# Loads that cast to bf16 in the DMA, transposes of contiguous blocks, and an output phase two batches behind, in an attention and MoE kernel

## The chip, the cores and the metric

The kernel runs on one core of a Trainium2 chip. The metric is the device time of one execution in microseconds (us). A core has these engines: PE (TensorE, matmuls), DVE (VectorE), ACT (ScalarE), POOL (GpSimd) and SP (SyncE, which here only issues DMAs). 16 DMA engines move data for all of them. Executions of the kernel before mostly lie between 346 and 353 us. Some runs fell in a slow state, most of them with a lower granted PE clock; ratios leave them out, but for one, and the medians quoted count every run.

## The reference, cut to what matters

```python
batch, n_heads, seq, head_dim = (8, 8, 576, 64);  n_pack = 32
def sm_attn(qq, kk, vv):                       # softmax attention
    s = scale * np.matmul(qq, kk.transpose(0, 1, 3, 2))
    s = s - np.max(s, axis=-1, keepdims=True)
    a = np.exp(s)
    a = a / (np.sum(a, axis=-1, keepdims=True) + 1e-09)
    return np.matmul(a, vv)
p_packed = sm_attn(p, k, v)                    # 32 packed rows attend to 576 tokens
out = sm_attn(q, p_packed, p_packed)           # 576 tokens attend to the 32 rows
# ... x is out as (4608, 512)
h = x @ w_in                                   # 512 -> 2048
g = h * np.cos(h)
return g @ w_out                               # 2048 -> 512, fp32
```

Inputs and output are fp32; q, k and v are 1.18 MB per batch each. The kernel computes in bf16. It folds the second attention into w_in: PPW = p_packed @ w_in (32 rows per head), so h is the normalised weights a2n times PPW.

## The kernel before: the parts that the argument touches

A stage is one pass of the loop over batches. Stage s does the second attention of batch s (`s2`, `sums2`, `normalise`), the first attention of batch s + 1 (`s1`, a transpose of its weights a1 to a1T, `pp`, `ppw`), the h phase of batch s, and output matmuls of batch s - 1, spread as filler for PE (`fill(n)` emits n of them). The transposes of k, q and a1 go through DMA transposes that SP issues in program order. Tokens lie as `(p c)`: 96 partitions with 6 tokens each.

```python
raw_pool = ctx.enter_context(tc.tile_pool(name="raw", bufs=3))
def load(n, b, eng):                           # fp32, as it lies in memory
    t = raw_pool.tile([TP, H, C * D], FP32, name="raw", tag="raw")
    eng.dma_start(out=t, in_=srcs[n][b].rearrange("h (p c) d -> p h (c d)", c=C))
    raws[n, b] = t
def cast(n, b, eng, c0=0, c1=C):               # to bf16, (h c) -> (c h)
    ...
def xbar(n, b):                                # DMA transpose of q or k
    t = new_xT(n, b)
    nc.sync.dma_start_transpose(out=t.rearrange("p c a x -> p (c a) x"),
                                in_=bf[n, b].rearrange("p c x -> p (c x)"))
# ... cut
for s in range(1, B):
    nxt = s + 1 < B
    if s > 1:
        set_filler(s - 1)
        nc.scalar.preload_act_table_set(EXP_SET)
    s2(s)
    fill(7)
    if nxt:
        s1(s + 1)
        a1_xbar(s + 1)
        xbar("q", s + 1)
        if s + 2 < B:
            if ("k", s + 2) not in bf:
                cast("k", s + 2, G)
            xbar("k", s + 2)
    fill(3)
    sums2(s, 0)
    # ... cut
    for n, b in loads:                         # v and q of s + 2, k of s + 3
        load(n, b, G)
    # ... cut: 16 x h_mm; pp at 4, ppw at 7 and 11; casts on POOL at 8, 11, 14
set_filler(B - 1)
fill(1000)
```

The softmax here doesn't subtract the row's maximum and nothing guards it: scores larger than these inputs give would overflow.

Of the kernel before, what the change touches and what calls it, by code (L numbers as in the profile page):

```python
# [15 lines left out]
def kernel(  # L16
# [10 lines left out]

# [13 lines left out]
    raw_pool = ctx.enter_context(tc.tile_pool(name="raw", bufs=3))  # L41
    bf_pool = ctx.enter_context(tc.tile_pool(name="bf", bufs=1))
    att_pool = ctx.enter_context(tc.tile_pool(name="att", bufs=1))
    a2n_pool = ctx.enter_context(tc.tile_pool(name="a2n", bufs=2))
    ppw_pool = ctx.enter_context(tc.tile_pool(name="ppw", bufs=2))
    g_pool = ctx.enter_context(tc.tile_pool(name="g", bufs=2))
# [7 lines left out]
    ctx.enter_context(tc.manual_schedule())  # L54

# [5 lines left out]
    P2 = const.tile([128, B, 4, NP], BF16, name="P2")  # L61
# [3 lines left out]
    ppT = [const.tile([128, 4, NP], BF16, name=f"ppT{i}") for i in range(2)]  # L65
# [3 lines left out]
    raws, bf, xT, a1T, sums1, r1, rs1 = {}, {}, {}, {}, {}, {}, {}  # L69
    a2u, lns, a2n, PPW = {}, {}, {}, {}  # L70

# [3 lines left out]
    def load(n, b, eng):  # L75
        t = raw_pool.tile([TP, H, C * D], FP32, name="raw", tag="raw")
        eng.dma_start(out=t, in_=srcs[n][b].rearrange("h (p c) d -> p h (c d)", c=C))
        raws[n, b] = t

    def cast(n, b, eng, c0=0, c1=C):  # L80
        if (n, b) not in bf:
            bf[n, b] = bf_pool.tile([TP, C, H * D], BF16, name=n + "bf", tag=n + "bf", bufs=2 if n == "v" else 1)
        sv = raws[n, b].rearrange("p h (c d) -> p c h d", c=C)[:, c0:c1]
        dv = bf[n, b].rearrange("p c (h d) -> p c h d", h=H)[:, c0:c1]
        if eng is nc.scalar:
            nc.scalar.copy(out=dv, in_=sv)
        else:
            eng.tensor_copy(out=dv, in_=sv)  # L88

    def new_xT(n, b):  # L90
        xT[n, b] = att_pool.tile([128, C, 4, TP], BF16, name=n + "T", tag=n + "T")
        return xT[n, b]

    def xbar(n, b):
        t = new_xT(n, b)
        nc.sync.dma_start_transpose(out=t.rearrange("p c a x -> p (c a) x"),
                                    in_=bf[n, b].rearrange("p c x -> p (c x)"))

    def pe_T(n, b, i, eng):
        if i == 0:  # L100
            new_xT(n, b)
        ps = psa(BF16)
        for j in range(2):
            for hp in range(4):
                o = (j * 4 + hp) * TP
                nc.tensor.transpose(ps[:, 0, o:o + TP],
                                    bf[n, b][:, 2 * i + j, hp * 128:(hp + 1) * 128], ident[0:TP, 0:TP])
        dst = xT[n, b][:, 2 * i:2 * i + 2].rearrange("p c a x -> p (c a x)")
        sv = ps[:, 0, 0:8 * TP]
        if eng is nc.scalar:  # L110
            nc.scalar.copy(out=dst, in_=sv)
        else:
            nc.vector.tensor_copy(out=dst, in_=sv)

    def pack_p(b0, b1):
        n = b1 - b0
        ps = psa(BF16)
        flat = ps.rearrange("p a x -> p (a x)")
        for g in range(2 * n):
            nc.tensor.transpose(flat[:, g * 128:(g + 1) * 128],  # L120
                                p_bf[:, 2 * b0 + g].rearrange("p t d -> p (t d)"), ident)
        v4 = flat[:, 0:2 * n * 128].rearrange("p (a o n) -> p a o n", o=2, n=NP)
        dst = P2[:, b0:b1].rearrange("p b a x -> p (b a) x")
        nc.vector.tensor_copy(out=dst[0:64], in_=v4[0:64, :, 0, :])
        nc.vector.tensor_copy(out=dst[64:128], in_=v4[64:128, :, 1, :])

    def scores(lhs, rhs):
        ps = [psa(), psa()]
        for half in range(2):
            for hp in range(4):  # L130
                for par in range(2):
                    r = slice(64 * par, 64 * par + 64)
                    nc.tensor.matmul(ps[par][32 * hp:32 * hp + 32, half, 0:HS], lhs[r, hp, :],  # L133
                                     rhs[r, 3 * half:3 * half + 3, hp, :], start=True, stop=True)
        return ps

    def s1(b):
        ps = scores(P2[:, b], xT["k", b])
        sums1[b] = small.tile([128, 2], FP32, name="sums1")
        for par in range(2):  # L140
            nc.scalar.activation(  # L141
                out=a1[b % 2][:, par, :, 0:TP].rearrange("p (t c) x -> p t c x", t=2),
                in_=ps[par][:, :, 0:HS].rearrange("p t (c x) -> p t c x", c=3),
                func=AF.Exp, scale=scale, accum_out=sums1[b][:, par:par + 1])
        r1[b] = small.tile([128, 2], FP32, name="r1")
        rs1[b] = small.tile([128, 2], FP32, name="rs1")
        nc.vector.reciprocal(r1[b], sums1[b])  # L147
        nc.vector.tensor_scalar(out=rs1[b], in0=r1[b], scalar1=scale, scalar2=None, op0=ALU.mult)

    def new_a1T(b):  # L150
        a1T[b] = att_pool.tile([128, 2, C, 128], BF16, name="a1T", tag="a1T")
        return a1T[b]

    def a1_xbar(b):
        t = new_a1T(b)
        nc.sync.dma_start_transpose(out=t.rearrange("p a c x -> p (a c) x"),
                                    in_=a1[b % 2].rearrange("p a c x -> p (a c x)"))

    def a1_pe(b, engs):
        t = new_a1T(b)  # L160
        ps = psa(BF16)
        for par in range(2):
            for c in range(C):
                nc.tensor.transpose(ps[0:TP, par, c * 128:(c + 1) * 128], a1[b % 2][:, par, c, 0:TP], ident)
            dst = t[0:TP, par].rearrange("p c x -> p (c x)")
            sv = ps[0:TP, par, 0:C * 128]
            if engs[par] is nc.scalar:
                nc.scalar.copy(out=dst, in_=sv)
            else:
                nc.vector.tensor_copy(out=dst, in_=sv)  # L170

    def pp(b):
        ps = psa()
        for hp in range(4):
            for c in range(C):
                nc.tensor.matmul(ps[:, 0, hp * 64:(hp + 1) * 64], bf["v", b][:, c, hp * 128:(hp + 1) * 128],  # L176
                                 a1T[b][0:TP, :, c, 32 * hp:32 * hp + 32], start=(c == 0), stop=(c == C - 1))
        pv = ps[:, 0, 0:256].rearrange("p (a x) -> p a x", a=4)
        t = ppT[b % 2]
        nc.vector.tensor_copy(out=t[0:64], in_=pv[0:64, :, 0:32])  # L180
        nc.vector.tensor_copy(out=t[64:128], in_=pv[64:128, :, 32:64])

    def ppw(b, n0, cnt, engs):
        if b not in PPW:
            PPW[b] = ppw_pool.tile([128, 2, DF], BF16, name="PPW", tag="PPW")
        ps = [psa(), psa()]
        for j in range(cnt):
            for hp in range(4):
                for par in range(2):
                    r = slice(64 * par, 64 * par + 64)  # L190
                    nc.tensor.matmul(ps[par][32 * hp:32 * hp + 32, j, :], ppT[b % 2][r, hp, :],  # L191
                                     w_in_bf[r, hp, (n0 + j) * 512:(n0 + j + 1) * 512], start=True, stop=True)
        for par in range(2):
            dst = PPW[b][:, par, n0 * 512:(n0 + cnt) * 512].rearrange("p (j x) -> p j x", j=cnt)
            sv = ps[par][:, 0:cnt, :]
            if engs[par] is nc.scalar:
                nc.scalar.activation(out=dst, in_=sv, func=AF.Copy, scale=r1[b][:, par:par + 1])  # L197
            else:
                nc.vector.tensor_scalar(out=dst, in0=sv, scalar1=r1[b][:, par:par + 1], scalar2=None, op0=ALU.mult)  # L199

    def s2(b):
        a2u[b] = att_pool.tile([128, 2, S], BF16, name="a2u", tag="a2u")
        ps = scores(ppT[b % 2], xT["q", b])
        for par in range(2):
            nc.scalar.activation(out=a2u[b][:, par].rearrange("p (t x) -> p t x", t=2),
                                 in_=ps[par][:, :, 0:HS], func=AF.Exp, scale=rs1[b][:, par:par + 1])

    def sums2(b, par):
# [3 lines left out]
        for half in range(2):  # L212
            nc.tensor.matmul(ps[:, half, 0:HS], ones_blk, a2u[b][:, par, half * HS:(half + 1) * HS],
                             start=True, stop=True)
        nc.scalar.activation(out=lns[b][:, par].rearrange("p (t x) -> p t x", t=2),
                             in_=ps[:, :, 0:HS], func=AF.Ln)

    def normalise(b):
        a2n[b] = a2n_pool.tile([128, 2, S], BF16, name="a2n", tag="a2n")
        for par in range(2):  # L220
            nc.scalar.activation(out=lns[b][:, par], in_=lns[b][:, par], func=AF.Exp, scale=-1.0)  # L221
        for par in range(2):
            nc.vector.tensor_tensor(out=a2n[b][:, par], in0=a2u[b][:, par], in1=lns[b][:, par], op=ALU.mult)  # L223
# [3 lines left out]
    def h_mm(b, fc):  # L227
# [5 lines left out]
        for par in range(2):  # L233
            for half in range(2):
                nc.tensor.matmul(ps[:, half, 0:HS], PPW[b][:, par, fc * 128:(fc + 1) * 128],  # L235
                                 a2n[b][:, par, half * HS:(half + 1) * HS], start=(par == 0), stop=(par == 1))
# [213 lines left out]
```

## Time and profile before

| | before |
|---|---|
| time, median | 351.73 us (350.46 to 353.24) |
| span of the profiled run, mean granted clock | 350.8 us, 0.919 |
| first h matmul (batch 0) | 32.4 us |
| h phase of batch 0 | 32.4 to 55.3 us |
| stages 2 to 5, from one `s2` to the next | 33.7, 42.0, 43.2, 35.4 us |
| PE waiting for DMA transposes | 26.9 us for a1T, 18.5 us for kT |
| last output alone | 17.9 us, then 4.6 us to the end |

These are lines of the page of the kernel before: span, busy time of each engine with its share, three rows of the strip in 40 slices (each digit tenths; PEclk is the granted clock), and the chain that ended last, by engine and by line.

```profile
span 350.8 us, 4906 instructions
PE 258.3 (74%) x1960; PEld 136.0 (39%) x1960; DVE 161.1 (46%) x239; ACT 185.8 (53%) x264; POOL 96.3 (27%) x79
PE   0545869640298898898088971999688999999994
PEclk9999998985589999999569995899989999999998
DMA  7979999999889969979991399715991181121132
PE 41%; DMA 38%; ACT 11%; DVE 5%; issue 3%; POOL 2%; SPq 0%; POOLq 0%; ACTq 0%
PE ot L270 22%; DMA a1T<-a 17%; PE psA L235 12%; DMA raw<-in_k_dram 7%; DMA kT<-kbf 6%; DMA raw<-in_q_dram 5%; ACT PPW L197 4%; DVE gT L242 3%; DMA raw<-in_v_dram 3%; PE psA L191 3%; ACT cosT L239 3%; PE psA L176 2%; PE psA L133 1%; DVE a2n L223 1%; ACT L378 1%
```

PE is the busiest engine and yet idle for a quarter of the span. The holes in its row after the first slice lie where the DMA row is at 8 or 9, and a lower clock follows them. The chain in order of time names the culprits (some of its pieces: start, duration, what it was):

```profile
72.24 22.30 DMA kT<-kbf
124.93 9.93 DMA a1T<-a
157.53 18.70 DMA a1T<-a
199.77 18.41 DMA a1T<-a
243.45 11.98 DMA a1T<-a
```

The last a1T, in a stage without loads, landed in 3.8 us. What is different in the others is seen in the timeline of POOL and of SP (start, duration, engine, line, operation):

```profile
155.25 0.79 POOL L77 DMA_DIRECT2D raw<-in_v_dram  x1
156.02 0.78 POOL L77 DMA_DIRECT2D raw<-in_q_dram  x1
156.79 0.78 POOL L77 DMA_DIRECT2D raw<-in_k_dram  x1
157.53 10.70 SPq L156 DMA_TRANSPOSE a1T<-a  x1
168.34 7.80 SPq L96 DMA_TRANSPOSE qT<-qbf  x1
```

POOL issues 3.5 MB of loads, and a microsecond later SP issues the small transpose for which the stage waits.

### The profile page before, as it was taken

Reading aid. Unit: us, or ns where it says so; the run is one execution under the profiler, and the core shown is the slowest. Engines: PE = TensorE matmul, PEld = TensorE weight load, DVE = VectorE, ACT = ScalarE, POOL = GpSimd, SP = SyncE. Lnnn points to the kernel's source line nnn. Section 1 sums busy time; section 2 is a strip of 40 time slices with the busy share of each in tenths; the row PEclk is TensorE's granted clock in tenths of the full one; section 3 lists DMA queues with packets and bytes.
Section 4 is the critical chain, followed back from the end, with each engine's and each line's share of the span. In section 5 each row is a group of like instructions: output and inputs, shape, how many; then the busy total and the mean of one; then the engine's idle time right before and its main releaser. Section 6 shows DMA issues by size and latency. Waiting matters only on the chain.

```text
span 350.8 us, 4906 instructions
## 1 busy us (share of the span) xinstructions
PE 258.3 (74%) x1960; PEld 136.0 (39%) x1960; DVE 161.1 (46%) x239; ACT 185.8 (53%) x264; POOL 96.3 (27%) x79
## 2 busy tenths in 40 slices
PE   0545869640298898898088971999688999999994
PEld 0432336410054344444044441454344454456541
DVE  1553676420057645745036450562537376638500
ACT  1407535440177884688027960469636976787400
POOL 1383026762232550390007500092006000000000
PEclk9999998985589999999569995899989999999998
DMA  7979999999889969979991399715991181121132
GB/s 174 226 111 204 211 219 218 248 210 105 92 177 222 244 128 216 193 197 245 203 200 33 94 227 213 171 29 135 213 195 30 45 161 30 30 62 37 54 88 61
DMA packets 55910, 52.22 MB, mean 149 GB/s; under 512 B 39392, under 2 KB 45792, under 8 KB 55888
## 3 DMA queue, kind: packets, MB, share of 16 engines
q0 software_dynamic: 10064, 29.43, 40.2%
q1 hardware_dynamic: 45824, 22.49, 33.6%
q8 instruction: 15, 0.25, 0.3%
q14 instruction: 7, 0.06, 0.1%
HBM read 37.22 MB, written 9.44 MB: 133 GB/s over the span
## 4 chain that ended last, share of the span: by engine, by line
PE 41%; DMA 38%; ACT 11%; DVE 5%; issue 3%; POOL 2%; SPq 0%; POOLq 0%; ACTq 0%
PE ot L270 22%; DMA a1T<-a 17%; PE psA L235 12%; DMA raw<-in_k_dram 7%; DMA kT<-kbf 6%; DMA raw<-in_q_dram 5%; ACT PPW L197 4%; DVE gT L242 3%; DMA raw<-in_v_dram 3%; PE psA L191 3%; ACT cosT L239 3%; PE psA L176 2%; PE psA L133 1%; DVE a2n L223 1%; ACT L378 1%
## 5 line engine op out<-in xcount | busy, mean ns | idle before, releaser
L239 ACT ACTIVATE cosT<-psA,pihalf 128x576 bf16<-128x576 f32 x128 | 93.9, 740 | 84.4 <-PE psA L235 83.2
L270 PE MATMUL ot<-w_out_bf,gT 128*128 128x512 bf16 x512 | 137.1, 393 | 0.0
L242 DVE TENSOR_TENSOR gT<-psA,cosT 128x576 bf16<-128x576 f32 x128 | 95.9, 756 | 50.4 <-ACT cosT L239 49.7
L235 PE MATMUL psA<-a2n,PPW 128*128 128x288 bf16 x512 | 91.9, 308 | 13.9 <-ACT PPW L197 6.7
L235 PEld LDWEIGHTS <-PPW 128*128 128x128 bf16 x512 | 52.9, 105 | 57.8 <-issue 16.4
L270 PEld LDWEIGHTS <-gT 128*128 128x128 bf16 x512 | 49.0, 100 | 47.8 <-issue 11.9
L246 POOL COPY joint<-gT 128x512 bf16<-128x512 bf16 x16 | 9.7, 612 | 169.0 <-DVE gT L242 169.0
L176 PE MATMUL psA<-a1T,vbf 96*128 96x64 bf16 x192 | 8.6, 210 | 33.2 <-DMA a1T<-a 26.9
L199 DVE TENSOR_SCALAR PPW<-psA,r 128x1024 bf16<-128x1024 f32 (+1 forms) x21 | 22.9, 1103 | 8.8 <-PE psA L191 8.5
L88 POOL CAST vbf<-raw 96x3072 bf16<-96x3072 f32 x8 | 22.0, 2747 | 14.6 <-DMA raw<-in_v_dram 14.6
L88 POOL CAST kbf<-raw 96x3072 bf16<-96x3072 f32 x7 | 19.2, 2745 | 17.1 <-DMA kT<-kbf 13.3
L88 POOL CAST qbf<-raw 96x3072 bf16<-96x3072 f32 (+1 forms) x8 | 19.8, 2479 | 12.8 <-DMA qT<-qbf 7.3
L147 DVE RECIPROCAL r<-sums 128x2 f32<-128x2 f32 x8 | 1.3, 166 | 44.3 <-ACT a L141 44.3
L176 PEld LDWEIGHTS <-vbf 96*128 96x128 bf16 x192 | 8.0, 109 | 34.8 <-issue 34.3
L191 PE MATMUL psA<-w_in_bf,ppT 64*32 64x512 bf16 x256 | 17.6, 401 | 5.1 <-DVE gT L242 3.3
L141 ACT ACTIVATE a<-psA 128x576 bf16<-128x576 f32 x16 | 10.2, 646 | 20.4 <-PE psA L133 20.4
L133 PE MATMUL psA<-kT,P 64*32 64x288 bf16 x128 | 5.3, 321 | 20.6 <-DMA kT<-kbf 18.5
L223 DVE TENSOR_TENSOR a2n<-a2u,lns 128x576 bf16<-128x576 bf16 x16 | 11.4, 755 | 18.9 <-ACT lns L221 18.9
L197 ACT ACTIVATE PPW<-psA,r 128x1024 bf16<-128x1024 f32 (+1 forms) x15 | 16.3, 1084 | 7.1 <-PE psA L191 7.1
L277 ACT COPY osb<-ot 128x512 f32<-128x512 f32 x18 | 10.4, 580 | 17.3 <-PE ot L270 17.1
L275 DVE COPY osb<-ot 128x512 f32<-128x512 f32 x18 | 12.3, 684 | 13.2 <-PE ot L270 13.2
L180 DVE CAST ppT<-psA 64x128 bf16<-64x128 f32 x8 | 2.3, 282 | 32.2 <-PE psA L176 32.2
(55 smaller groups left out, 172.5 us busy)
## 6 DMA issues: line engine op xcount, KB each, us to landing
raw<-in_k_dram POOLq DMA_DIRECT2D x7, 1152.0 KB, 18.8
raw<-in_v_dram POOLq DMA_DIRECT2D x7, 1152.0 KB, 10.3
raw<-in_q_dram POOLq DMA_DIRECT2D x7, 1152.0 KB, 15.0
out_dram<-osb SPq DMA_DIRECT2D x24, 192.0 KB, 2.3
out_dram<-osb SPq DMA_DIRECT2D x24, 128.0 KB, 2.4
w_in_bf<-in_moe_w_in_dram POOLq DMA_DIRECT2D x4, 512.0 KB, 8.5
w_out_bf<-in_moe_w_out_dram POOLq DMA_DIRECT2D x4, 512.0 KB, 17.0
out_dram<-osb SPq DMA_DIRECT2D x24, 64.0 KB, 2.0
```

The costliest lines, as they stand in the source:

```text
L88: eng.tensor_copy(out=dv, in_=sv)
L176: nc.tensor.matmul(ps[:, 0, hp * 64:(hp + 1) * 64], bf["v", b][:, c, hp * 128:(hp + 1) * 128], a1T[b][0:TP, :, c, 32 * hp:32 * hp + 32], s ...
L191: nc.tensor.matmul(ps[par][32 * hp:32 * hp + 32, j, :], ppT[b % 2][r, hp, :], w_in_bf[r, hp, (n0 + j) * 512:(n0 + j + 1) * 512], start=Tru ...
L197: nc.scalar.activation(out=dst, in_=sv, func=AF.Copy, scale=r1[b][:, par:par + 1])
L199: nc.vector.tensor_scalar(out=dst, in0=sv, scalar1=r1[b][:, par:par + 1], scalar2=None, op0=ALU.mult)
L223: nc.vector.tensor_tensor(out=a2n[b][:, par], in0=a2u[b][:, par], in1=lns[b][:, par], op=ALU.mult)
L235: nc.tensor.matmul(ps[:, half, 0:HS], PPW[b][:, par, fc * 128:(fc + 1) * 128], a2n[b][:, par, half * HS:(half + 1) * HS], start=(par == 0) ...
L239: nc.scalar.activation(out=csv, in_=ps[:, :, 0:HS], func=AF.Sin, bias=pihalf)
L242: nc.vector.tensor_tensor(out=gT[b][:, fc, :].rearrange("p (t x) -> p t x", t=2), in0=ps[:, :, 0:HS], in1=csv, op=ALU.mult)
L270: nc.tensor.matmul(ps, w, w_out_bf[:, fc, :], start=(fc == 0), stop=(fc == NFC - 1))
L275: nc.vector.tensor_copy(out=osb, in_=ps)
L277: nc.scalar.copy(out=osb, in_=ps)
```

## The change

The intent: no casts on engines, since DMAs issued by POOL can cast; with the cast gone, q and k are transposed as they lie, in 24 contiguous blocks of 128 columns, each holding an even and an odd token of one head. So the halves of the PE rows now hold token parity instead of head parity, and `P2` and `ppT` are held on both halves. A one-element copy, the gate, lets POOL issue a stage's loads only after a1T has landed. Batches 0 and 1 have no output filler: output runs two batches behind.

```diff
-    raw_pool = ctx.enter_context(tc.tile_pool(name="raw", bufs=3))
+    vp_pool = ctx.enter_context(tc.tile_pool(name="vp", bufs=2))
-    g_pool = ctx.enter_context(tc.tile_pool(name="g", bufs=2))
+    g_pool = ctx.enter_context(tc.tile_pool(name="g", bufs=3))
@@ load and cast
+    def load(n, b):
+        bf[n, b] = bf_pool.tile([TP, H, C * D], BF16, name=n + "bf", tag=n + "bf")
+        G.dma_start(out=bf[n, b], in_=srcs[n][b].rearrange("h (p c) d -> p h (c d)", c=C))
+    def permute_v(b, eng=G):
+        vp[b] = vp_pool.tile([TP, C, H * D], BF16, name="vp", tag="vp")
+        copy(eng, vp[b].rearrange("p c (h d) -> p c h d", h=H),
+             bf["v", b].rearrange("p h (c d) -> p c h d", c=C))
@@ scores: row tile e is the parity of the token, not of the head
-                    r = slice(64 * par, 64 * par + 64)
-                    nc.tensor.matmul(ps[par][32 * hp:32 * hp + 32, half, 0:HS], lhs[r, hp, :],
-                                     rhs[r, 3 * half:3 * half + 3, hp, :], start=True, stop=True)
+                    r = slice(64 * e, 64 * e + 64)
+                    h = 2 * x + y
+                    nc.tensor.matmul(t[32 * x:32 * x + 32, e, 0:HS], lhs[r, h, :],
+                                     rhs[r, 3 * h:3 * h + 3, :], start=True, stop=True)
@@ start: k, q of batches 0, 1 and k of 2 are transposed on PE
+    dup_p(2, 16, V)                            # ahead of the h phase of batch 0
+    for n in range(4):
+        for fc in range(4 * n, 4 * n + 4):
+            h_mm(0, fc)()
+            if fc == 4 * n + 1 and n < 3:
+                ppw(0, n + 1, 1, (V, ACT), O)
     ... (preparation of batches 1 and 2, h phase of batch 1, without filler)
+    permute_v(2)
     ...
+    set_filler(0)
@@ the loop
-    for s in range(1, B):
+    for s in range(2, B):
-            set_filler(s - 1)
+            set_filler(s - 2)
-            a1_xbar(s + 1)
             xbar("q", s + 1)
             if s + 2 < B:
                 xbar("k", s + 2)
+            a1_xbar(s + 1)
+            G.tensor_copy(out=gate, in_=a1T[s + 1][0:1, 0, 0, 0:1])
     ...
-    set_filler(B - 1)
+    for b in (B - 2, B - 1):
+        set_filler(b)
     fill(1000)
```

## The prediction

> **What bounds the kernel now** (the page, the chain of waits, windows of 10 us).
> 1. Start, 0 to 55 us. The first h matmul starts at 32.4: k lands at 8.9, casts and transposes follow, pp waits until 22.4 behind a DVE cast of q, and w_in is issued only at 19.7. The h phase of batch 0 takes 23 us, with gaps of 1 to 2.7 us at each PPW eviction.
> 2. DMA stalls, 72 to 260 us. The chain holds 38% DMA: a1T 17%, k loads 7%, kT 6%. fp32 loads and SP's transposes collide: one kT took 22.3 us to land (PE idle 76 to 94.6); a1T took 9.9, 18.7, 18.4, 12.0 us in loaded stages, 3.8 in the last, where no loads run. PE is busy 1.7 to 5.6 us of 10 in the windows at 160, 170, 210 and 250. Such stages last 41 to 42 us.
> 3. Clean stages, PE-bound: stage 6 takes 34.5 us (274.9 to 309.4); the final outputs are solid PE (out matmul 0.215 us at full clock), then 4 us of tail.
>
> **What changes.**
> - 24 casts on engines vanish (POOL 60 us at 2.74 each). The weights are already loaded with a cast: from 24 to 42 us the queue moved 204 GB/s counted in bf16, so 408 of source, against 225 for fp32 loads. A load of 1.18 MB should take 3.3 us instead of 5.2 (estimate).
> - The Trainium skill, "DMA: Bandwidth & Descriptors" (Rules for kernel authors), says that all queues share the same 16 engines; the trace agrees: a1T's landing depends on loads, as above. The gate copy on POOL holds a batch's loads until a1T has landed, so they no longer collide: the main gain. q's and k's transposes now go ahead of a1's: 3.5 + 3.0 + 3.8 us (clean durations), so a1T lands about 11 us into a stage, just when pp is due.
> - Added, off the critical path: a permutation of v per batch (about 2.7 us on POOL), two small ACT copies for ppT (0.3 us each).
> - Transposes and scores keep counts and shapes: no change of PE time.
> - Output two batches behind: h(0) and h(1) have no filler and become ACT/DVE-bound (16 x 0.76 plus PPW), but the 20 us wait for kT(2) goes: it is transposed on PE.
>
> **Sum, us.** First h matmul at 24; h(0) 16.5 (PPW now in the O pool); preparation of batches 1 and 2, 17; h(1) 16.5; first outputs and PPW(2) 8; stages 2 to 7: 29, 34.5, 31, 34.5, 31, 27; last two outputs 144 x 0.215 = 31; tail 4.5. Total about 301. Of the 51 saved, 30 to 35 are a1T and kT stalls, the rest the start.
>
> **What would show it.** POOL busy from 96 to about 45; the chain's DMA share from 38% to under 12%; a1T lands in under 7 us; stages 3 to 6 take 30 to 36 us each; first h matmul at 22 to 26; PE's share 82 to 86%; the two-output ending solid PE.
>
> **What would make it wrong.** Cast loads of 768-byte rows taking 5 us or more: then k(s+2) is late and a1's transpose, queued behind it on SP, stalls pp. The throttle: h(0) and h(1) without filler may draw the half clock seen at 50 to 54 and 76 to 95; then each takes 3 to 5 us longer. POOL's order (joint copies, permutation, gate, issues) delaying loads in stage 2. Faster, if the stages' overhead over PE's sum (5 us) shrinks too.
>
> Chances: faster by over 2% 0.96, within 2% 0.02, slower 0.02.

## The result, and the profile after

The changed kernel took 305.4 us in the median (304.68 to 306.81), beside 352.4 us for the kernel before in the same rounds; the ratio is 0.8678, 95% interval 0.8627 to 0.8729. A ratio here is the mean time of one kernel's fast runs over that of the other's of the same rounds, so it isn't quite the ratio of the medians that are quoted. The output is correct.

The lines of the page after, which answer to those of before:

```profile
span 303.9 us, 4986 instructions
PE 257.9 (85%) x1996; PEld 136.8 (45%) x1996; DVE 157.5 (52%) x243; ACT 190.8 (63%) x285; POOL 55.8 (18%) x67
PE   0766877978599678999998899999998999999993
PEclk9999796559869999999999999999999999999999
DMA  7999409999199993989189929891740111222222
PE 54%; ACT 17%; DVE 11%; DMA 10%; POOL 3%; issue 2%; SPq 0%; ACTq 0%; DVEq 0%; POOLq 0%
```

PE's busy time hasn't changed (258.3 and 257.9); the zeros in the middle of its row are gone, and DMA's share of the chain fell from 38% to 10%. The start is not free of half clock: the 5s in the eighth and ninth slices are new places. The chain in order of time has these a1T left:

```profile
99.71 3.77 DMA a1T<-a
159.75 3.80 DMA a1T<-a
189.41 3.88 DMA a1T<-a
```

The same stage in the timeline of SP and of POOL shows the new order: transposes of q, k, a1, and the loads only behind the gate.

```profile
153.42 3.01 SPq L93 DMA_TRANSPOSE qT<-qbf  x1
156.53 3.11 SPq L93 DMA_TRANSPOSE kT<-kbf  x1
159.75 1.45 SPq L144 DMA_TRANSPOSE a1T<-a  x1
163.66 0.18 POOL L394 COPY gate<-a1T 1x1 bf16<-1x1 bf16 x1 [8.72 <-DMA a1T<-a]
164.14 0.77 POOL L84 DMA_DIRECT2D vbf<-in_v_dram  x1 [0.30 <-POOL gate L394]
```

Stages 2 to 5 now take 28.6, 32.0, 29.8 and 31.5 us, though a stage's filler isn't quite the same: output lies one batch further behind, so stages with 64 and with 80 output matmuls change places, and stage 2 has only what is left of batch 0's 64.

### The profile page after: what moved, and what is told of

Read it like the earlier page. It is cut to its first block, busy times and chain, and to the rows that moved or that the text cites. A ratio compares the mean times of both kernels' runs of the same rounds, so it can differ in the third digit from the quotient of the medians.

```text
span 303.9 us, 4986 instructions
## 1 busy us (share of the span) xinstructions
PE 257.9 (85%) x1996; PEld 136.8 (45%) x1996; DVE 157.5 (52%) x243; ACT 190.8 (63%) x285; POOL 55.8 (18%) x67
## 4 chain that ended last, share of the span: by engine, by line
PE 54%; ACT 17%; DVE 11%; DMA 10%; POOL 3%; issue 2%; SPq 0%; ACTq 0%; DVEq 0%; POOLq 0%
PE ot L262 28%; PE psA L227 15%; DMA p_raw<-in_p_dram 6%; DVE gT L234 6%; ACT cosT L231 5%; ACT PPW L189 4%; DMA a1T<-a 4%; PE psA L183 3%; DVE a2n L215 3%; PE psA L160 2%; ACT lns L207 2%; PE psA L124 2%; PE psA L102 2%; ACT lns L213 1%; ACT L381 1%
## 5 line engine op out<-in xcount | busy, mean ns | idle before, releaser
L262 PE MATMUL ot<-w_out_bf,gT 128*128 128x512 bf16 x512 | 130.9, 384 | 0.0
L191 DVE TENSOR_SCALAR PPW<-psA,r 128x1024 bf16<-128x1024 f32 x12 | 15.4, 1284 | 9.9 <-PE psA L183 9.8
L77 POOL COPY vp<-vbf 96x3072 bf16<-96x3072 bf16 x7 | 19.2, 2749 | 4.0 <-DMA vbf<-in_v_dram 4.0
L189 ACT ACTIVATE PPW<-psA,r 128x1024 bf16<-128x1024 f32 x12 | 13.4, 1113 | 8.7 <-PE psA L183 8.7
L262 PE MATMUL ot<-w_out_bf,joint 128*128 128x512 bf16 x64 | 16.4, 379 | 0.0
L160 PE MATMUL psA<-a1T,vp 96*128 96x64 bf16 x192 | 8.7, 211 | 8.9 <-POOL vp L77 3.3
L170 ACT CAST ppT<-psA 64x128 bf16<-64x128 f32 x16 | 4.2, 260 | 17.4 <-DVE ppT L166 14.7
L183 PE MATMUL psA<-w_in_bf,ppT 64*32 64x512 bf16 x192 | 11.7, 400 | 2.7 <-DVE gT L234 2.6
L160 PEld LDWEIGHTS <-vp 96*128 96x128 bf16 x192 | 7.8, 110 | 10.8 <-POOL vp L77 5.4
L197 ACT ACTIVATE a2u<-psA,rs 128x576 bf16<-128x576 f32 x16 | 11.0, 736 | 2.4 <-PE psA L124 2.2
```

The source lines that it names most:

```text
L77: eng.tensor_copy(out=out, in_=in_)
L160: nc.tensor.matmul(ps[:, 0, hp * 64:(hp + 1) * 64], vp[b][:, c, hp * 128:(hp + 1) * 128], a1T[b][0:TP, :, j, 32 * hp:32 * hp + 32], start= ...
L183: nc.tensor.matmul(ps[y][32 * x:32 * x + 32, j, :], ppT[b % 2][r, 2 * x + y, :], w_in_bf[r, x, (n0 + j) * 512:(n0 + j + 1) * 512], start=T ...
L189: ACT.activation(out=dst, in_=sv, func=AF.Copy, scale=r1[b][:, y:y + 1])
L191: V.tensor_scalar(out=dst, in0=sv, scalar1=r1[b][:, y:y + 1], scalar2=None, op0=ALU.mult)
L197: ACT.activation(out=a2u[b][:, y].rearrange("p (e x) -> p e x", e=2), in_=ps[y][:, :, 0:HS], func=AF.Exp, scale=rs1[b][:, y:y + 1])
```

## The experiments

The theory after the result (A) was the prediction's: a1T was late because loads met its transpose on the shared DMA engines, and the gate cured that. The rival (B): loads were too heavy, and halving what they write did it. Both parts can be put into the kernel before alone, and the gate can be taken out of the changed kernel. Everything that ran gave correct results.

### The gate alone, in the kernel before

```diff
+        if nxt and loads:
+            G.tensor_copy(out=gate, in_=a1T[s + 1][0:1, 0, 0, 0:1])
         for n, b in loads:
             load(n, b, G)
```

> The kernel before, with one instruction of the change alone: the one-element copy on POOL that holds a stage's loads until a1T has landed. Theory A (the stalls come from loads that collide with a1's transpose on the 16 DMA engines): a1T lands in under 6 us in stages 2 to 5 (before 9.9 to 18.7), those stages take 34 to 36 us, the kernel 325 to 333 us. Theory B (the loads are too heavy, and cheaper loads made the gain): holding them back only moves the wait to q's and k's transposes or to the casts; the kernel stays within 2% of 352.

Measured: 322.19 us in the median, ratio 0.9253 (0.9174 to 0.9331); one of four runs was slow (337.5) and isn't counted in the ratio. a1T landed in 3.8 to 3.9 us in every stage, and stages 2 to 5 took 32.1, 28.4, 31.2 and 30.9 us, shorter than expected. The waits of PE for transposes (engine, line, what for: total us, times, longest) of this kernel:

```profile
PE psA L134 <- DMA kT<-kbf: 15.9, 2, 15.4
```

and of the kernel before:

```profile
PE psA L176 <- DMA a1T<-a: 26.9, 4, 11.1
PE psA L133 <- DMA kT<-kbf: 18.5, 1, 18.5
```

The wait for a1T is gone entirely; the wait for kT, at the start of stage 1, stays. k's transposes now meet the loads and land in 15.4 to 23.0 us, but after stage 1 PE waits no more than 0.5 us for them: k is needed one stage later. Theory A holds for a1T. One instruction of one element is worth 7.5% here.

### The cast alone, in the kernel before

```diff
-        t = raw_pool.tile([TP, H, C * D], FP32, name="raw", tag="raw")
+        t = raw_pool.tile([TP, H, C * D], BF16, name="raw", tag="raw")
@@ the first three loads
-        load(n, 0, nc.sync)
+        load(n, 0, G)
```

The engine copies stay and only permute. That the first loads must go to POOL too follows the Trainium skill, "DMA: Bandwidth & Descriptors" (SWDGE vs HWDGE vs iDMA), which has the cast during a DMA on GpSimd's path only; no run here tried another.

> The kernel before, with the cast moved into the DMA and nothing else: the raw tile is bf16, so every load is issued by POOL and writes half the bytes; the engine casts stay as permuting copies. Theory A: loads still collide with a1's transpose for some 10 us, a1T lands in 7 to 13 us, the kernel takes 335 to 345. Theory B: a1T lands in under 6 us and the kernel takes 325 or less.

Measured: 320.03 us, ratio 0.9217 (0.9133 to 0.9301). PE's waits for transposes:

```profile
PE psA L176 <- DMA a1T<-a: 16.0, 4, 6.8
PE psA L133 <- DMA kT<-kbf: 1.8, 1, 1.8
```

Neither theory foretold this. a1T still landed in 8.0 to 14.4 us in the four loaded stages of the chain, as A had it and against B; but the time lies where B had it. What A had left out is the start (by the beginning of stage 2 the profile is 23.3 of its 33.2 us ahead; with the gate alone it was 1.1 of 32.9): the wait for kT of batch 2 fell from 18.5 to 1.8 us, and the first h matmul comes at about 25.5 us instead of 32.4. The casting load itself is cheap: in the stage of the changed kernel at 164 us, v, q and k landed 2.9 us apart (from issue times and times to landing), against 5.1 us apart for the first three fp32 loads before, which SP issued. The issuer isn't the reason: three fp32 loads that POOL issued in the kernel before landed 5.1 us apart as well (at 136.1, 141.2 and 146.3 us).

### Both, in the kernel before

The two edits above together.

> The kernel before with both the gate and the casting loads. Theory A: the gate has already taken the stalls of stages 2 to 5, so the cast adds only the start and the wait for kT of batch 2 (some 5 to 10 us): 317 to 328 us. Theory B: the two add up only if loads still bind, then 315 or less.

Measured: 297.13 us, ratio 0.8555 (0.8414 to 0.8697). Two of the four runs were slow (299.7 and 299.1), and here the ratio must count at least one of them: the fast ones (293.2 and 295.2), over any fast run of the kernel before (346.3 to 350.3), give at most 0.8526. Their means give 294.2 / 348.1 = 0.845, which rests on two runs. The same kernel again in a later job:

> The same kernel as b_cast_gate again, so that it stands beside the others on one chip. Expected: a ratio of 0.84 to 0.86 to before (293 to 299 us), within 1% of the changed kernel with one batch behind, and faster than the changed kernel's 305.

Measured: 298.24 us, ratio 0.8445 (0.8362 to 0.8528), one of five runs slow. Neither theory's numbers held: the two gains add up in full (0.9253 x 0.9217 = 0.8529), since the gate cures a1T and the cast the start. In the first profile PE waits for no transpose at all; in the second for kT once more, 3.3 us. So **two small edits to the kernel before are worth at least as much as the whole change** (0.8678). The rest of the change then gives nothing net: it must hold losses as large as its gains. No run tries the layout (contiguous transposes) alone.

### The changed kernel without its gate

```diff
-            G.tensor_copy(out=gate, in_=a1T[s + 1][0:1, 0, 0, 0:1])
```

> The changed kernel without the gate. Theory A: loads start 5 to 10 us earlier in a stage and meet the transposes; a1T lands in 6 to 12 us instead of 3.8, and the kernel takes 312 to 325 us. Rival: the single buffers of q and k (a load waits until the transpose has read its buffer) and the cheap loads order the traffic well enough without it: within 1% of 305.

Measured: 348.63 us, ratio 1.0007 (0.9907 to 1.0107), one of four runs slow. All of the gain is gone. a1T lands in 7.8 to 10.6 us in the loaded stages, as A expected; the loss is larger than A expected, and the trace has a second delay: a1's transpose is also issued late, 10.6 to 16.5 us into a stage instead of 8.4 to 9.5, behind those of q and k, which the loads slow down as well. PE's wait:

```profile
PE psA L160 <- DMA a1T<-a: 41.0, 4, 15.7
```

In the changed kernel it is this:

```profile
PE psA L160 <- DMA a1T<-a: 3.2, 3, 1.8
```

38 us more of waiting, for 43 us more of time. The rival (single buffers order the traffic well enough) falls. The order that the change gave SP seems to make the gate indispensable: in the kernel before, where a1 goes first and PE's waits for a1T were 16.0 us with the casting loads, the same gate was worth some 26 us (means of fast runs, 320.1 and 294.2). That it is the order is argued, not shown: no run has the changed kernel with a1 first and without the gate.

### One batch behind

What does the change lose? A candidate (theory C) is the output phase: with no filler in the first two batches, PE idles early, and two outputs in a row are left at the end, when ACT and DVE have nothing to do.

```diff
@@ ahead of the h phase of batch 0
+    for n in range(4):
+        load_w_out(n)
@@ preparation of batch 1, with filler; batch 1's h phase moves into the loop
+    set_filler(0)
+    fill(8)
     pe_T("k", 1)
     ...
-    for s in range(2, B):
+    for s in range(1, B):
-            set_filler(s - 2)
+            set_filler(s - 1)
@@ end
-    for b in (B - 2, B - 1):
-        set_filler(b)
+    set_filler(B - 1)
```

Moved along with it: PPW of batch 1 goes through the larger PSUM tiles, a1 of batch 2 through a DMA transpose, v of batch 1 is permuted on DVE. The run doesn't tell these apart from the delay.

> The changed kernel with its output phase one batch behind again: w_out is loaded after q of batch 1, outputs of batch 0 fill PE during the preparation of batches 1 and 2 and the h phase of batch 1. Theory C (two batches behind leaves PE idle early and puts a second output of 14 to 17 us, in which ACT and DVE idle, at the end): 293 to 299 us, the pure output ending shrinks from 32 to about 18 us. Rival D (the layout and the start make the gain, and the delay by two batches is needed to hide the loads of w_out and of k of batch 2): 305 or slower, with a wait for w_out or kT early.

Measured: 293.97 us, ratio 0.8363 (0.829 to 0.8435). The pure output ending shrank from 32.0 to 17.9 us. That is all of the gain: the last h matmul ends at 267.1 us in the changed kernel and at 268.1 here, although the second has done 64 more output matmuls by then. The clock seems to be part of why they fit in. Stretches of the changed kernel (start and end; length, then busy us of PE, PEld, DVE, ACT and POOL with counts; granted clock, DMA share, GB/s):

```profile
40.90:62.90 22.00, 15.54 (x204) 10.93 (x202) 11.12 (x21) 14.39 (x26) 9.38 (x10) 0.65 0.91 140
77.10:90.30 13.20, 9.94 (x88) 3.74 (x86) 4.85 (x8) 4.50 (x6) 7.11 (x6) 0.74 0.58 83
```

The preparation in the run with one batch behind:

```profile
42.30:64.30 22.00, 18.77 (x236) 10.32 (x238) 11.63 (x21) 14.16 (x25) 6.46 (x6) 1.00 0.98 137
```

Both take 22 us up to the h phase of batch 1, but the second also holds 45 output matmuls (20 ahead of the loop, 25 in it, by the code), at full clock. The Trainium skill, "TensorE: Matmul & The Clock Gate" (What's actually happening), says that PE's activity sets the clock and that it falls after an idle window of about 3.4 us. The direction agrees: filler kept it at 1.00. In the changed kernel it fell in the middle of the preparation (the same columns; the last three are granted clock, DMA share, GB/s):

```profile
46.00:47.00 1.00, 0.87 (x12) 0.57 (x10) 0.55 (x2) 0.38 (x2) 1.00 (x1) 1.00 0.84 60
47.00:48.00 1.00, 0.00 (x0) 0.00 (x0) 1.00 (x2) 0.79 (x1) 1.00 (x2) 0.73 1.19 174
48.00:49.00 1.00, 0.52 (x11) 0.55 (x12) 0.34 (x1) 0.00 (x0) 1.00 (x2) 0.50 1.32 206
```

The window's length agrees too: in all 14 traces, every stretch between two changes of the clock is a whole number of 3.41 us. That the window must be idle doesn't. The falls inside the changed kernel, at 30.4, 47.5 and 81.6 us, followed windows in which PE had been busy for 1.05, 1.74 and 0.77 of 3.41 us; the fall at 51.6 us in the kernel before followed one with 1.73. So a window in which PE works for half of the time can be enough. It isn't a sharp limit: a window with 1.59 us (from 249.6 us in the kernel before) brought no fall. Some of PE's work at 47 us is transposes, whose weight for the clock no run here tells apart; there are none at 30.4 and 51.6.

Theory C stands, as far as a run with these other edits can show it; D (the delay hides the loads of w_out) falls.

### Two waits near the start

Both are plain in the trace. DVE waits for p until 26.8 us, ahead of the h phase of batch 0 (the chain has 19.6 us of "DMA p_raw" there); and PE waits 3.3 us at 79 us for the permutation of v of batch 2, which POOL starts only behind the joint copies of batch 1.

```diff
@@ a_p
-    dup_p(2, 16, V)
     ... (h phase of batch 0)
+    dup_p(2, 16, V)
     pack_p(1, 8)
@@ a_v2
-    permute_v(2)
+    permute_v(2, V)
```

> The changed kernel with the cast of the other batches' p moved on DVE from ahead of the h phase of batch 0 to behind it: it waits until 26.8 us for p, and DVE runs in order. If that wait is on the critical path, the h phase of batch 0 takes 15 to 16 us instead of 18 and the kernel 302 to 304 us; if the phase is bound by ACT and DVE anyway, within 1 us of 305.

> The changed kernel with the permutation of v of batch 2 on DVE instead of POOL, where it waits behind the joint copies of batch 1: PE waited 3.3 us for it at 79 us and then ran at half clock. Expected: pp of batch 2 starts 3 us earlier, the kernel takes 301 to 303 us; if the first outputs merely move into the gap, within 1 us of 305.

> One batch behind, and the cast of p behind the h phase: the two gains add up if both are on the critical path: 290 to 297 us, 2 to 3 us below the run with one batch behind alone.

Measured: 307.16 us (ratio 0.8727) for p; 304.97 us (0.8664) for v; 295.15 us (0.8388) for the edit of p together with one batch behind. None is a gain. Moving p shortened the h phase of batch 0 as expected (the second preload of ACT's table came at 38.6 us instead of 41.7), but then PE itself waits for the cast:

```profile
40.95 1.67 PE L112 MATMUL psA<-ident,p_bf 128*128 128x128 bf16 x14 [3.11 <-DVE p_bf L304]
```

That is the timeline of PE in this run; the bracket is the idle time and what ended it. The wait only changed its engine, and the granted clock fell to half during it, between 40 and 41 us, some 7 us earlier than in the changed kernel. With v on DVE, pp of batch 2 started 1.9 us earlier (80.3 instead of 82.2), but stage 3 started at 119.0 instead of 119.7 us by ACT's table loads: most of it went into stage 2, which began 4.4 us earlier (85.8 instead of 90.3) and where the chain now contains 2% "DMA qT<-qbf": the q of batch 3 landed only 0.9 us earlier (90.7 instead of 91.6). A wait seen in the trace isn't yet a cost.

### a1's transpose first on SP again

The change put a1's transpose behind q's and k's. PE waited 3.2 us for a1T in the changed kernel, 7.9 us with one batch behind (the expectations' 5.6 and 8.7 us also hold its waits for the first batches' a1T, which DVE and ACT copy):

```profile
PE psA L160 <- DMA a1T<-a: 7.9, 3, 4.2
```

```diff
-            xbar("q", s + 1)
-            if s + 2 < B:
-                xbar("k", s + 2)
             a1_xbar(s + 1)
+            xbar("q", s + 1)
+            if s + 2 < B:
+                xbar("k", s + 2)
             G.tensor_copy(out=gate, in_=a1T[s + 1][0:1, 0, 0, 0:1])
```

> The changed kernel with a1's transpose ahead of q's and k's on SP, as before the change. If the order costs: PE's waits for a1T (5.6 us in total) vanish, kT lands in 10 to 17 us as loads now meet it, without anybody waiting, and the kernel takes 300 to 303 us. If the order protects k's transpose from the loads, k comes late for the next stage: 305 to 310 us.

> One batch behind and a1's transpose first on SP: PE waited 8.7 us for a1T in the run with one batch behind (294), 2.5 in the kernel before with gate and cast. If that wait is all on the critical path, 286 to 290 us; if the loads now collide with k's transpose to the same effect, 293 to 296.

Measured: 300.84 us (0.8563, 0.8513 to 0.8613) in the changed kernel; 282.54 us (0.8051, 0.8004 to 0.8099) with one batch behind, the best. kT now lands in 10.9 to 17.0 us in the faster one, among loads, and PE waits for none of them. The gain with one batch behind is larger than the 7.9 us of waiting that the profile showed: stage 1 alone, where PE had waited 4.2 us, ended 5.5 us earlier by ACT's table loads (at 84.4 instead of 89.9). The clock can be a part of it: with q and k first it fell to half from 72.7 to 76.1 us, right after that wait, with PE busy throughout, which costs up to 1.7 us (estimate); with a1 first it stays at 1.00 until 278 us. How the rest of the surplus arises isn't settled.

This run also shows what the rest of the change is worth once the delay and SP's order are taken back. It took 282.8 us in the mean, beside 296.7 for the fast runs of the kernel before with gate and cast in the same job: 4.7% less. The gain lies ahead of stage 2, which starts at 83.5 us instead of 99.2; from there on the two profiles run level (stages 2 to 5 take 120.5 and 120.9 us).

The last run asked whether the loads should miss k's transpose as well:

```diff
                 xbar("k", s + 2)
-            G.tensor_copy(out=gate, in_=a1T[s + 1][0:1, 0, 0, 0:1])
+                G.tensor_copy(out=gate, in_=xT["k", s + 2][0:1, 0, 0:1])
```

> As the run before, but the gate waits for k's transpose, so that a1T comes first and the loads still meet no transpose. All three transposes land in under 8 us; loads start 6 us later. If it is the overlap that costs and loads have slack, 285 to 290 us and not slower than with the gate on a1T; if loads have no slack, v or k is late and it takes 3 us or more longer than that.

Measured: 284.14 us (0.8081, 0.8035 to 0.8128). kT lands in 4.9 to 5.4 us, and nothing is gained: a slow transpose costs nothing where nobody waits. Here the transfer to protect was the one that PE waited for next, not the one that was slowed most.

The runs for gate and cast were one job on one chip, the others two further jobs on another chip; each is set against its own runs of the kernel before.

## Why the prediction was right or wrong

The time was right: 301 predicted, 305.4 measured. There is a slip in it: the terms of the sum, as listed, make 304.5, not 301. And the close total is partly luck: the terms miss by 13 us upwards and by 14 us downwards.

| part, us | predicted | measured |
|---|---|---|
| first h matmul | 24 | 22.9 |
| h phase of batch 0 | 16.5 | 18.0 |
| preparation of batches 1 and 2 | 17 | 22.0 |
| h phase of batch 1 | 16.5 | 14.2 |
| first outputs, PPW(2) | 8 | 13.2 |
| stages 2 to 7 together | 187 | 176.8 |
| last two outputs | 31 | 32.0 |
| tail | 4.5 | 4.9 |

- **The bound** was read correctly. Loads and SP's transposes collided, and the gate cured it: a1T lands in 3.7 to 4.8 us ("under 7"), the chain's DMA share is 10% ("under 12%"), PE's share 85% ("82 to 86%"); of stages 3 to 6 two fell just short of "30 to 36 us" (32.0, 29.8, 31.5, 29.2). The run without the gate shows that it carries the whole gain of the changed kernel.
- **The cast load** was estimated at 3.3 us from the weights' loads; the prediction's own 408 GB/s would have given 2.9 for 1.18 MB, and the trace has 2.9. The feared case, 5 us or more, didn't come.
- **The Trainium skill**, "DMA: Bandwidth & Descriptors" (Rules for kernel authors), on the shared 16 engines: the runs agree. The same a1 transpose took about 3.8 us without loads (at most 5.8), mostly 7.8 to 14.4 among casting ones (3.8 where they were issued a microsecond behind it), 7.3 to 18.7 among fp32 ones.
- **The split of the gain** ("30 to 35 are a1T and kT stalls, the rest the start") was too low for the stalls: PE's waits for transposes fell from 45.4 us to 3.2, by 42 us. By stretches of the profile, the start up to stage 2 saved 29.6 us, stages 2 to 7 saved 31.6, and the longer ending lost 14.1. But the prediction called the gate "the main gain" and gave the cast no share of its own. Alone, in the kernel before, the cast was worth 7.8% and the gate 7.5%.
- **"POOL busy from 96 to about 45"**: 55.8. By the prediction's own terms (96, less 60 for casts, plus seven permutations of 2.7) it should have been 55.
- **"Added, off the critical path: a permutation of v per batch"**: PE did wait 3.3 us for one of them. Taking that wait away gained nothing measurable, so the statement held for the time, not for the trace.
- **Mis-sized terms**: the preparation (22.0 for 17) and the first outputs (13.2 for 8) ran at a granted clock of 0.65 and 0.74, and the second also held the wait for v. The throttle was named as a risk, but for the h phases. The six stages were 10 us shorter together than predicted, which by luck made up for it. They were taken too long at the source: from one `s2` to the next, the clean stage 6 of the kernel before lasts 31.7 us (274.2 to 305.9), not 34.5.
- **The step that failed**: "Output two batches behind: h(0) and h(1) have no filler ... but the 20 us wait for kT(2) goes." The wait went through the faster loads, as the run with the cast alone shows (18.5 to 1.8 us); transposing k of batch 2 on PE and the delay weren't needed for it. The delay, which the prediction booked as the price for losing that wait, costs without a return: with one batch behind the kernel is at 0.8363 instead of 0.8678.
- **"a1T lands about 11 us into a stage, just when pp is due"**: it landed about 13 us into it (163.5 us in the stage that starts at 150.8), and PE waited at most 1.8 us. Having a1 first is worth a further 1.3% (0.8563), and more with one batch behind.

## What to carry to other kernels

When a small transfer that everybody waits for shares the DMA engines with bulk loads that nobody needs yet, hold the loads with a real dependency on the small transfer and issue the small one first; check both by taking them out again. Try the cheap parts of a rewrite alone in the old kernel before crediting the rewrite: here two edits of a few lines did as well as all of it, and two parts that nobody had booked as costs, the delay of the output phase and the order of the transposes, ate what the rest had gained. Filler work belongs in the earliest idle time of PE, both for its own sake and because here broken activity lowered the clock of what followed (0.65 and 0.74 beside 1.00).

## What the Trainium skill lacked or had wrong

- "DMA: Bandwidth & Descriptors" (Rules for kernel authors) says that a transpose next to ordinary DMAs needs nothing. For correctness every run agrees. For time no page has the price: the same transpose took 3.8 us alone and mostly 7.3 to 18.7 us among loads.
- The same page (Measured) gives 341 GB/s for a load of 1 MB, and no figure for loads that cast. Here fp32 loads of 1.18 MB in rows of 1536 bytes, issued by SP or by POOL, landed 5.1 us apart (about 231 GB/s), and casting ones, issued by POOL, 2.9 us apart (about 407 GB/s of source): the cast made a load faster.
- "TensorE: Matmul & The Clock Gate" (What's actually happening) gives an idle window of about 3.4 us as what lowers the clock. The window's length is right (3.41 us here), but it need not be idle: PE was busy for 1.05, 1.74 and 0.77 us of the windows before the three falls inside the changed kernel. Another section (A second HAM failure mode: psum-queue depth-cycling) does tell of short idle times between groups of matmuls that make the clock swing; no page says how much work keeps a window from counting as idle.
